# A fused convolution and channel mix: reordering the first bundles of work

## The chip, the cores and the metric

The kernel runs on one core of a Trainium2 chip. A core has five engines that run side by side, each through its own instruction queue in order: TensorE (PE) multiplies matrices and loads their stationary operand (PEld), VectorE (DVE) and ScalarE (ACT) work element by element, GpSimd (POOL) issues most of the loads here, and SyncE (SP) issues the transfers of the results. Sixteen DMA engines move data between HBM and the on-chip memory SBUF. TensorE writes its results into PSUM, which VectorE and ScalarE read.

The metric is the time of one execution on the device in microseconds (us), the median of several runs.

## The reference

The input `x` is `[8, 4160, 192]`: 8 sequences of 4160 positions with 192 channels. First comes a causal convolution along the positions, with 7 taps per head (8 heads of 24 channels), the taps normalised by a softmax. Its result goes through a channel mix:

```python
xk = mu_k * x + (1.0 - mu_k) * x_prev      # x_prev: the position before
xr = mu_r * x + (1.0 - mu_r) * x_prev
k = np.maximum(xk @ w_k, 0.0)              # 192 -> 1024
v = k * k @ w_v                            # 1024 -> 192
r = 1.0 / (1.0 + np.exp(-(xr @ w_r)))      # 192 -> 192
return (r * v).astype(np.float32)
```

Here `x` is already the convolution's result, called `y` below.

## The kernel before

The eight sequences are worked through as four pairs. For each pair the kernel convolves, transposes `y` so that channels lie on partitions (`yT`), mixes, and multiplies.

**Convolution.** Positions are cut into blocks of 120, blocks into groups. Pair 0 has groups 0 to 5 of 3, 4, 4, 5, 10 and 9 blocks; later pairs have four groups each. The convolution is a matmul with a banded matrix `toe`; its input `xb` is loaded by `load_x` through POOL's queue into one of three buffers (`x_tile` takes one). Groups 0 to 2 are convolved whole (`conv_small`: matmuls at L312, copies out of PSUM by ACT at L320). From group 3 on a group is cut into units, each in two halves on TensorE (`conv_mm`, L291); after the second half ACT copies the unit out (`conv_out`, L336). Between the halves ACT's sequencer puts a marker instruction (`clobber_nop`, L299), for which the second half waits.

**Transposing.** Groups 0 to 3 are transposed on TensorE (`tr_first`, and `tr`, L380, four blocks to one PSUM buffer) and copied to `yT` by DVE (L389). From group 4 on `y` goes to HBM (`y_write`, L359) and comes back through a transposing DMA (`y_read`, L367), both in SP's queue.

**Mixing.** A step is a piece of 512 positions of both sequences (256 for the first and the last step of pair 0). `diff` (L433) is the difference of `yT` to its neighbour, `scale` (L464) multiplies one third of the channels by `mu`, `add_y` (L470) adds `yT` again. `mix(s, 0)` gives `xk`, `mix(s, 1)` gives `xr`. All are on DVE, whose order is written out in tables.

**Products.** A step of 512 has eight K slots; a slot is six matmuls (`k_mm`, L490), three thirds of the channels for each of the two sequences, with one block of 128 columns of `w_k` over 512 positions of `xk`, then a ReLU on ACT (`k_relu`, L519) and a square on DVE (`k_square`, L533). A step of 256 has four slots, each covering 256 of the 1024 columns of `w_k`, so slots 0 and 1 of step 0 use columns 0 to 511. For each half step ("quad") there is one R (`r`, 12 matmuls, L564, and a sigmoid on ACT, L572) and one V (`v_rows`, two halves of 32 matmuls, L592), multiplied by `v_out` on DVE (L608) and sent out by SP (L616).

**Order.** Everything stands in an order written out by hand. The K slots are taken four at a time, a *bundle*. `bundle_first` is bundle 0; `bundle_rest` writes the others: four K slots, up to two convolution units, an R and a V of earlier steps. Tables (`early`, `first`, `rq`, `mix_a`, `mix_b`, `mix_c`, `late`) say which other calls stand at which place in which bundle; `run(table, b)` writes them. `at(table, b, fn, ...)` enters a call. Units of group 3 are in bundle 1, of group 4 in bundles 2 and 3, of group 5 in bundles 4 and 5: two per bundle. Later bundles have one unit at most.

PSUM is one ring of four buffers: each K slot, unit, R, V and each transposition of four blocks takes the next buffer, and waits until the buffer's last user has been read out. `xb`, `xk`, `xr` and `k_sb` are rings of three, two, two and four buffers.

The loads at the start stand in POOL's queue in this order: `xb` of group 1, `w_k` in four pieces (`load_wk`: channels 0 to 127 twice, once for each sequence's partitions, then channels 128 to 191 twice), `xb` of groups 2 and 3, `w_r`, `w_v`, then in bundle 1 `xb` of groups 4 and 5.

Of the kernel before, what the change touches and what calls it, by code (L numbers as in the profile page):

```python
# [14 lines left out]
def kernel(  # L15
# [11 lines left out]
    nc = tc.nc  # L27
# [5 lines left out]
    P = 128  # L33
# [65 lines left out]
    def x_tile(g):  # L99
        p, blk0, nb, _, _ = groups[g]  # L100
        xb = three.tile([P, GB, 2, D], BF16, tag="xb", name="xb")
        xbs[g] = xb
        if g > 4:

            nc.vector.memset(xb[0:1, 0, 0, 0:2], 0.0)  # L105
        if blk0 == 0:
            nc.gpsimd.memset(xb[0:32, 0, :, :], 0.0)  # L107
        if blk0 + nb == NBLK:
            nc.gpsimd.memset(xb[:, nb - 1, :, :], 0.0)
# [72 lines left out]
    def load_thirds(w, m, n, cs=slice(0, NC)):  # L182
        for st in range(2):
            nc.gpsimd.dma_start(
                out=w[st * Q : (st + 1) * Q, cs, :],
                in_=bass.AP(
                    tensor=m.tensor,
                    offset=m.offset + cs.start * Q * n,
                    ap=[[n, Q], [Q * n, cs.stop - cs.start], [1, n]],
                ),  # L190
            )

    def load_wk():
        load_thirds(wk, moe_w_k, DF, slice(0, 2))
        load_thirds(wk, moe_w_k, DF, slice(2, 3))

    def load_wr():
        load_thirds(wr, moe_w_r, D)

    def load_wv():  # L200
        nc.gpsimd.dma_start(out=wv, in_=moe_w_v.rearrange("(f p) d -> p f d", p=P))
# [170 lines left out]
    def tr(g, j):  # L372

        p, blk0, nb, _, _ = groups[g]
        ps = ring.tile([P, 2, 2 * BANK], BF16, tag="k", name="ps_t")
        todo = range(4 * j, min(nb, 4 * j + 4))
        view = ps[:, :, 0 : 6 * BLK].rearrange("p b (c i t) -> p b c i t", c=3, i=2)
        for c in range(3):
            for i in todo:
                nc.tensor.transpose(  # L380
                    out=view[:, (i - 4 * j) // 2, c, i % 2, :],
                    in_=ys[g][c][:BLK, i, :] if g < 3 else ys[g][:BLK, i, c * P : (c + 1) * P],
                    identity=ident[:BLK, :BLK],
                )

        for i in todo[::2]:
            n = min(2, nb - i)
            c0 = YC + (blk0 + i) * BLK
            nc.vector.tensor_copy(  # L389
                out=yTs[p][:, :, c0 : c0 + n * BLK].rearrange("p c (n t) -> p c n t", n=n),  # L390
                in_=view[:, (i - 4 * j) // 2, :, :n, :],
            )
# [122 lines left out]
    def k_relu(n):  # L515
        ps = k_ps.pop(n)
        k_sb = four.tile([P, 2 * STEP], BF16, tag="k_sb", name="k_sb")
        k_sbs[n] = k_sb
        nc.scalar.activation(out=k_sb, in_=ps.rearrange("p a b -> p (a b)"), func=AF.Relu)  # L519

    def k_square(n):
        s, j = slots[n]
        L = steps[s][2]
        k_sb = k_sbs.pop(n)
        if j == 0:
            k2s[s] = three.tile([P, NF, 2 * STEP], BF16, tag="k2", name="k2")
        nf = STEP // L
        i = k_sb
        o = k2s[s][:, j, :]
        if nf > 1:  # L530
            i = k_sb.rearrange("p (b f t) -> p f b t", b=2, f=nf)
            o = k2s[s][:, j * nf : (j + 1) * nf, 0 : 2 * L].rearrange("p f (b t) -> p f b t", b=2)
        nc.vector.tensor_tensor(out=o, in0=i, in1=i, op=ALU.mult)  # L533
# [108 lines left out]
    def at(table, b, fn, *a):  # L642
        table.setdefault(b, []).append((fn, a))
# [5 lines left out]
    def conv_half(unit, half):  # L649
        if unit is not None:  # L650
            conv_mm(*unit, half)
            if half == 1:
                conv_out(*unit, nc.scalar.copy)

    for g, (p, blk0, nb, fb, on_pe) in enumerate(groups):
        nx = 1 if g < 3 else len(conv_units(g))
        if g == 0:
            continue
        if g == 1:
            xs = []  # L660
        elif p == 0:
            xs = {2: [0], 3: [1, 1], 4: [2, 2, 3, 3], 5: [4, 4, 5, 5]}[g]
        else:
            xs = range(fb - 10, fb - 10 + nx)
        for i, b in enumerate(xs):
            if g == 2:
                at(late, b, conv, g, i)
            else:
                xt.setdefault(b, []).append((g, i))
        if on_pe:  # L670
            for j in range((nb + 3) // 4):
                at(first, g - 1, tr, g, j)
        else:
            at(late, xs[-1], y_write, g)

            at(late, xs[-1] + (1 if g < 6 else 2), y_read, g)
        if g > 3:

            b = {4: 1, 5: 1, 6: 2, 7: 8}.get(g)
            b = first_bundle[first_step[p]] + (-15, -11, -7, -3)[(g - 6) % 4] if b is None else b  # L680
            at(early, b, x_tile, g)
            at(early, b, load_x, g)
    for s, (p, t0, L, n0, ns) in enumerate(steps):
        fb = first_bundle[s]
        if s == 0:
            at(late, 0, mix, s, 1)
            continue
        if s == 1:
            at(mix_a, 0, diff, s)
            at(mix_a, 0, mix, s, 0)  # L690
            at(mix_a, 1, mix, s, 1)
        else:
            if s == 4:
                at(mix_a, fb - 1, diff, s)
            else:
                at(mix_c, fb - 2, diff, s)
            at(mix_a, fb - 1, scale, s, 0, 0)
            at(mix_b, fb - 1, scale, s, 0, 1, 2)
            at(mix_b, fb - 1, scale, s, 1, 0)
            at(mix_c, fb - 1, add_y, s, 0)  # L700
            at(mix_a, fb, scale, s, 1, 1)
            at(mix_b, fb, scale, s, 1, 2)
            at(mix_b, fb, add_y, s, 1)
        if s == LAST - 1 or s < LAST and steps[s + 1][0] > p:
            at(late, fb - 1, keep_tail, p)
    for s, j, vb in quads:
        at(rq, vb - 1, r, s, j)
        if s == LAST:
            at(late, vb, v_last, s, j)
        else:  # L710
            vq.setdefault(vb, []).append((s, j))

    def run(table, b):
        for fn, a in table.get(b, ()):
            fn(*a)
# [5 lines left out]
    def prologue():  # L721
        nc.sync.dma_start(
            out=w_raw,
            in_=bass.AP(tensor=weight.tensor, offset=weight.offset, ap=[[0, P], [K, H], [1, K]]),
        )
        nc.vector.memset(x_f32[0:32, 0, :, :], 0.0)
        nc.vector.memset(ones_t, 1.0)
        for st in range(2):
            load_x_first(nc.scalar, 0, P, 1, groups[0][2], st, st + 1)
        load_x_first(nc.sync, 16, P, 0, 1, 0, 2)  # L730
        load_mu(0, moe_mu_k)
        load_x_first(nc.scalar, HALO, 16, 0, 1, 0, 2)
        nc.scalar.preload_act_table(AF.Exp)
        nc.vector.memset(zeros, 0.0)  # L734
        x_tile(1)
        nc.gpsimd.affine_select(
            out=ident,
            in_=ones_t,
            pattern=[[1, P]],
            compare_op=ALU.is_equal,  # L740
            fill=0.0,
            base=0,
            channel_multiplier=-1,
        )
        masks_band()
        load_x(1)
        load_wk()

        warm(ring.tile([P, 2, BANK], FP32, tag="k", name="warm"), WARM)
        x_tile(2)  # L750
        masks_mod8()
        softmax()
        make_toe()
        load_x(2)
        load_mu(1, moe_mu_r)
        conv(0, 0)
        tr_first()
        conv(1, 0)
        x_tile(3)
        load_x(3)  # L760
        load_wr()
        load_wv()

    def bundle_first(ns):
# [9 lines left out]
    def bundle_rest(b, ns):  # L774

        units = xt.get(b, []) + [None, None]
        quad = vq.get(b, [None])[0]
        for n in bundles[b - 1][2:] if b > 1 else ():
            k_square(n)
        run(mix_a, b)  # L780
        k_mm(ns[0])
        k_relu(ns[0])
        k_square(ns[0])
        run(mix_b, b)
        conv_half(units[0], 0)
        k_mm(ns[1])
        conv_half(units[0], 1)
        k_relu(ns[1])
        k_square(ns[1])
        run(rq, b)  # L790
        run(first, b)
        if quad:
            v_rows(*quad, 0)
        conv_half(units[1], 0)
        k_mm(ns[2])
        conv_half(units[1], 1)
        k_relu(ns[2])
        if quad:
            v_rows(*quad, 1)
        run(mix_c, b)  # L800
        k_mm(ns[3])
        k_relu(ns[3])
        if quad:
            v_out(*quad)
        run(late, b)
# [51 lines left out]
```

## Time and profile before

| | |
|---|---|
| median of 5 runs | 424.19 us (423.63 to 425.2) |
| profiled execution, its own time | 423.21 us |
| its span, first to last instruction | 421.5 us |
| TensorE busy | 407.5 us, 97% of the span |
| VectorE busy | 380.8 us, 90% |
| ScalarE busy | 347.5 us, 82% |
| chain that ended last, by line | V (L592) 38%, K (L490) 38%, R 7%, convolution 4%, loading `w_k` 2%, reading `yT` back 2% |

How to read it: busy times are those of one profiled execution. The chain that ended last is followed back from the last instruction, at each step to what released it; its shares say where the time went. A wait in brackets after an instruction is idle time of its engine, with the work that ended it. An instruction's line is that of the call that made it, so all K slots have one line. The profiled execution's own time is 1.71 us more than its span.

### The profile page before, as it was taken

The page shows a single profiled execution, that of the slowest core. Times are in us where ns is not written, and L with a number is a line of the kernel's source. Part 1 is how long each engine was busy: PE and PEld are TensorE (multiplying, and loading weights), DVE is VectorE, ACT ScalarE, POOL GpSimd, SP SyncE. Part 2 cuts the span into 40 slices and gives each one's busy share as a digit, 9 for nine tenths or more (in the row PEclk, how much of TensorE's full clock was granted, in tenths as well). Part 3 has the DMA queues.
Part 4 walks back from the last instruction along what each step waited for, and adds up shares of the span by engine and source line. Part 5 has one row for each costly group of instructions (what it writes and reads, how often), then busy time and mean ns, then how long its engine had stood idle before and what let it go on. Part 6 is the DMA issues. An engine that isn't in the chain of part 4 may idle for free.

```text
span 421.5 us, 15786 instructions
## 1 busy us (share of the span) xinstructions
PE 407.5 (97%) x6845; PEld 314.7 (75%) x6845; DVE 380.8 (90%) x678; ACT 347.5 (82%) x407; POOL 48.9 (12%) x73
## 2 busy tenths in 40 slices
PE   6779999999999999999999999999999999999995
PEld 3456768777877787787778777777877787777795
DVE  6897879998999999999999999999999999999983
ACT  5788988888988898888888888988898788777771
POOL 6550001202021010202003010200100000000000
PEclk9999999999999999999999999999999999999999
DMA  8997779959589793887869794695756484421123
GB/s 132 192 178 114 183 187 184 206 186 176 165 147 222 147 213 118 139 198 159 192 110 213 170 193 136 136 237 142 151 145 138 139 157 121 117 78 53 64 79 113
DMA packets 134502, 64.58 MB, mean 153 GB/s; under 512 B 85132, under 2 KB 134048, under 8 KB 134432
## 3 DMA queue, kind: packets, MB, share of 16 engines
q1 hardware_dynamic: 96050, 48.31, 44.6%
q0 software_dynamic: 37488, 14.66, 30.4%
q8 instruction: 53, 0.87, 0.9%
q10 hardware_dynamic: 894, 0.61, 0.5%
q14 instruction: 17, 0.14, 0.1%
HBM read 29.92 MB, written 36.99 MB: 159 GB/s over the span
## 4 chain that ended last, share of the span: by engine, by line
PE 89%; DVE 4%; DMA 4%; ACT 1%; POOL 1%; issue 1%; SPq 0%; ACTq 0%; DVEq 0%
PE ps_v L592 38%; PE ps_k L490 38%; PE ps_r L564 7%; PE ps_c L291 4%; DMA wk<-in_moe_w_k_dram 2%; DMA yT<-y_dram 2%; PE ps_v L547 1%; DVE k L533 1%; ACT k_sb L519 1%; DVE d L433 0%; DVE yT L389 0%; DVE xk L470 0%; DVE xk L464 0%; POOL xb L125 0%; DVE xr L464 0%
## 5 line engine op out<-in xcount | busy, mean ns | idle before, releaser
L519 ACT ACTIVATE k_sb<-ps_k 128x1024 bf16<-128x1024 f32 x260 | 260.9, 1038 | 55.5 <-PE ps_k L490 55.3
L490 PE MATMUL ps_k<-xk,wk 64*128 64x512 bf16 (+1 forms) x1632 | 200.9, 367 | 2.9 <-DVE xk L470 1.6
L533 DVE TENSOR_TENSOR k<-k_sb 128x1024 bf16<-128x1024 bf16 x260 | 177.7, 688 | 14.0 <-ACT k_sb L519 6.4
L592 PE MATMUL ps_v<-wv,k 64*128 64x192 bf16 x4032 | 188.8, 243 | 0.6 <-ACT k_sb L519 0.6
L592 PEld LDWEIGHTS <-k 64*128 64x128 bf16 x4032 | 172.4, 94 | 13.2 <-issue 0.6
L490 PEld LDWEIGHTS <-wk 64*128 64x128 bf16 x1632 | 87.1, 94 | 55.0 <-DVE xk L470 2.3
L608 DVE TENSOR_TENSOR o_sb<-ps_v,r_sb 128x768 f32<-128x768 f32 x64 | 61.2, 957 | 13.5 <-PE ps_v L592 9.0
L572 ACT ACTIVATE r_sb<-ps_r 128x768 bf16<-128x768 f32 x65 | 54.6, 840 | 0.0
L336 ACT CAST y<-ps_c 120x960 bf16<-120x960 f32 (+4 forms) x67 | 50.9, 787 | 4.3 <-PE ps_c L291 4.3
L125 POOL DMA_DIRECT2D xb<-in_x_dram x34 | 30.8, 909 | 196.8 <-PE ps_c L291 129.2
L564 PEld LDWEIGHTS <-xr 64*128 64x128 bf16 x780 | 36.0, 94 | 12.8 <-DVE xb L105 2.0
L564 PE MATMUL ps_r<-wr,xr 64*128 64x192 bf16 x780 | 43.8, 243 | 1.7 <-DVE xb L105 1.7
L291 PE MATMUL ps_c<-xb,toe 64*128 64x480 bf16 (+2 forms) x240 | 39.4, 335 | 0.0
L464 DVE TENSOR_SCALAR xr<-d,mu 128x512 bf16<-128x512 bf16 (+1 forms) x102 | 35.2, 348 | 0.0
L464 DVE TENSOR_SCALAR xk<-d,mu 128x512 bf16<-128x512 bf16 (+1 forms) x99 | 32.4, 356 | 0.1
L470 DVE TENSOR_TENSOR xr<-xr,yT 128x1536 bf16<-128x1536 bf16 (+1 forms) x33 | 31.0, 939 | 1.1
L433 DVE TENSOR_TENSOR d<-yT 128x1536 bf16<-128x1536 bf16 (+2 forms) x35 | 31.1, 888 | 0.8 <-DMA yT<-y_dram 0.6
L470 DVE TENSOR_TENSOR xk<-xk,yT 128x1536 bf16<-128x1536 bf16 (+1 forms) x32 | 30.2, 944 | 0.0
L291 PEld LDWEIGHTS <-toe 64*128 64x128 bf16 x240 | 13.3, 94 | 11.9 <-issue 0.3
L417 POOL COPY y_tail<-yT 128x195 bf16<-128x195 bf16 x4 | 1.8, 457 | 68.6 <-DMA yT<-y_dram 68.6
L719 PE MATMUL warm<-zeros,ones_t 128*128 128x512 bf16 x16 | 5.0, 480 | 1.8 <-DVE zeros L734 1.8
L107 POOL MEMSET xb<- 32x384 bf16 x3 | 1.2, 407 | 45.9 <-PE ps_k L490 43.7
(54 smaller groups left out, 64.0 us busy)
## 6 DMA issues: line engine op xcount, KB each, us to landing
out_dram<-o_sb SPq DMA_DIRECT2D x128, 192.0 KB, 2.9
y_dram<-y SPq DMA_DIRECT2D x10, 900.0 KB, 6.7
xb<-in_x_dram POOLq DMA_DIRECT2D x14, 480.0 KB, 8.9
xb<-in_x_dram POOLq DMA_DIRECT2D x6, 432.0 KB, 7.6
xb<-in_x_dram POOLq DMA_DIRECT2D x10, 192.0 KB, 5.0
y_dram<-y SPq DMA_DIRECT2D x3, 450.0 KB, 5.8
y_dram<-y SPq DMA_DIRECT2D x1, 810.0 KB, 6.0
xb<-in_x_dram POOLq DMA_DIRECT2D x2, 384.0 KB, 7.0
```

The source lines that it names most:

```text
L291: nc.tensor.matmul(out=banks[:, bank, :, :, k * G : (k + 1) * G], lhsT=toe[q, h, :], rhs=xbs[g][q, :nb, :, h * G : (h + 1) * G], start=hal ...
L336: copy(out=bass.AP(tensor=y.tensor, offset=y.offset + d0, ap=[y.ap[0], [d1 - d0, 2], [2 * D, nb], [Q, 2], [1, n]],), in_=bass.AP(tensor=ps ...
L433: nc.vector.tensor_tensor(out=shaped(s, diffs[s][:, cs, :L]), in0=y_of(s, cs, 1), in1=y_of(s, cs, 0), op=ALU.subtract)
L464: nc.vector.tensor_scalar(out=t[:, c, :L], in0=diffs[s][:, c, :L], scalar1=mu[:, i, c : c + 1], scalar2=None, op0=ALU.mult)
L470: nc.vector.tensor_tensor(out=o, in0=o, in1=y_of(s, sl, 0), op=ALU.add)
L490: nc.tensor.matmul(out=ps[:, i, f * L : (f + 1) * L], lhsT=wk[r, c, fs], rhs=xk[r, c, :L], start=c == 0 and f == 0, stop=c == NC - 1 and f ...
L519: nc.scalar.activation(out=k_sb, in_=ps.rearrange("p a b -> p (a b)"), func=AF.Relu)
L533: nc.vector.tensor_tensor(out=o, in0=i, in1=i, op=ALU.mult)
L564: nc.tensor.matmul(out=ps[:, i, k * D : (k + 1) * D], lhsT=xr[q, c, ts], rhs=wr[q, c, :], start=c == 0, stop=c == NC - 1,)
L572: nc.scalar.activation(out=r_sbs[s, j], in_=ps[:, :, 0 : 2 * D], func=AF.Sigmoid)
L592: nc.tensor.matmul(out=v_ps[s, j][:, bank, k * D : (k + 1) * D], lhsT=k2s[s][q, f, t * P : (t + 1) * P], rhs=wv[q, f, :], start=half == 0 ...
L608: nc.vector.tensor_tensor(out=o_sb.rearrange("p (b t) d -> p b (t d)", b=2), in0=v_ps.pop((s, j)), in1=r_sbs.pop((s, j)), op=ALU.mult,)
```

## The change

Six edits, all of which touch the start of the program and bundles 0 to 8.

- `load_wk` loads `w_k` by halves of its columns: two pieces for columns 0 to 511 (all 192 channels, once for each sequence's partitions), then two for columns 512 to 1023.
- Group 4's `x_tile` and `load_x` move from bundle 1 to the start, ahead of `load_wv`. Group 7's move from bundle 8 to bundle 7.
- `tr` writes its transposes in pairs of blocks, all three channel parts of a pair together. For group 1 the second pair is copied to `yT` by ACT instead of DVE.
- The table `first` (the transposes of groups 2 and 3) is run behind the first K slot and its ReLU instead of behind the second slot and R.
- Up to bundle 6, an R stands in the bundle of its V instead of one bundle earlier, so that bundle 6 holds two R. The mixes for R of steps 0, 1 and 2 stand later, those of step 1 in parts.
- Where a bundle has two units, the third of its K slots with its ReLU moves ahead of the second unit, and the second half of that unit behind V's second half.

```diff
     def load_wk():
-        load_thirds(wk, moe_w_k, DF, slice(0, 2))
-        load_thirds(wk, moe_w_k, DF, slice(2, 3))
+        for half in range(2):
+            h = slice(half * DF // 2, (half + 1) * DF // 2)
+            for st in range(2):
+                nc.gpsimd.dma_start(
+                    out=wk[st * Q : (st + 1) * Q, :, h],
+                    in_=bass.AP(
+                        tensor=moe_w_k.tensor,
+                        offset=moe_w_k.offset + h.start,
+                        ap=[[DF, Q], [Q * DF, NC], [1, DF // 2]],
+                    ),
+                )
...
-        for c in range(3):
-            for i in todo:
-                nc.tensor.transpose(
...
+        for i0 in todo[::2]:
+            for c in range(3):
+                for i in range(i0, min(nb, i0 + 2)):
+                    nc.tensor.transpose(
...
         for i in todo[::2]:
...
-            nc.vector.tensor_copy(
+            copy = nc.scalar.copy if g == 1 and i > 0 else nc.vector.tensor_copy
+            copy(
...
-        if g > 3:
-
-            b = {4: 1, 5: 1, 6: 2, 7: 8}.get(g)
+        if g > 4:
+
+            b = {5: 1, 6: 2, 7: 7}.get(g)
...
         if s == 0:
-            at(late, 0, mix, s, 1)
+            at(mix_c, 1, mix, s, 1)
             continue
         if s == 1:
             at(mix_a, 0, diff, s)
             at(mix_a, 0, mix, s, 0)
-            at(mix_a, 1, mix, s, 1)
+            at(mix_a, 1, scale, s, 1, 0)
+            at(mix_b, 1, scale, s, 1, 1)
+            at(late, 2, scale, s, 1, 2)
+            at(late, 2, add_y, s, 1)
         else:
-            if s == 4:
+            if s == 2:
+                at(mix_b, 1, diff, s)
+            elif s == 4:
                 at(mix_a, fb - 1, diff, s)
             else:
                 at(mix_c, fb - 2, diff, s)
             at(mix_a, fb - 1, scale, s, 0, 0)
             at(mix_b, fb - 1, scale, s, 0, 1, 2)
-            at(mix_b, fb - 1, scale, s, 1, 0)
             at(mix_c, fb - 1, add_y, s, 0)
-            at(mix_a, fb, scale, s, 1, 1)
+            if s == 2:
+                at(mix_a, fb, scale, s, 1, 0)
+                at(mix_b, fb, scale, s, 1, 1)
+            else:
+                at(mix_b, fb - 1, scale, s, 1, 0)
+                at(mix_a, fb, scale, s, 1, 1)
             at(mix_b, fb, scale, s, 1, 2)
             at(mix_b, fb, add_y, s, 1)
...
     for s, j, vb in quads:
-        at(rq, vb - 1, r, s, j)
+        at(rq, vb if vb < 7 else vb - 1, r, s, j)
...
         load_wr()
+        x_tile(4)
+        load_x(4)
         load_wv()
...
         k_mm(ns[0])
         k_relu(ns[0])
+        run(first, b)
         k_square(ns[0])
...
         run(rq, b)
-        run(first, b)
         if quad:
             v_rows(*quad, 0)
+        k_mm(ns[2])
+        k_relu(ns[2])
         conv_half(units[1], 0)
-        k_mm(ns[2])
-        conv_half(units[1], 1)
-        k_relu(ns[2])
         if quad:
             v_rows(*quad, 1)
+            conv_half(units[1], 1)
         run(mix_c, b)
         k_mm(ns[3])
+        if not quad:
+            conv_half(units[1], 1)
         k_relu(ns[3])
```

More of the change, by code (lines that the diff above doesn't have):

```diff
@@ L377, in tr @@
         view = ps[:, :, 0 : 6 * BLK].rearrange("p b (c i t) -> p b c i t", c=3, i=2)
-        for c in range(3):
-            for i in todo:
-                nc.tensor.transpose(
[L381 to L384, printed above, removed]
+        for i0 in todo[::2]:
+            for c in range(3):
+                for i in range(i0, min(nb, i0 + 2)):
+                    nc.tensor.transpose(
+                        out=view[:, (i - 4 * j) // 2, c, i % 2, :],
+                        in_=ys[g][c][:BLK, i, :] if g < 3 else ys[g][:BLK, i, c * P : (c + 1) * P],
+                        identity=ident[:BLK, :BLK],
+                    )
         for i in todo[::2]:
```

## The prediction

> **What bounds the kernel now.** I read the first part of the page, then busy time by stretches, then TensorE's waits, then the chain and the timeline of the first 65 us.
>
> ```profile
> span 421.5 us, 15786 instructions
> PE 407.5 (97%) x6845; PEld 314.7 (75%) x6845; DVE 380.8 (90%) x678; ACT 347.5 (82%) x407; POOL 48.9 (12%) x73
> ```
>
> TensorE is busy in 97% of the span. The stretches (columns: PE, PEld, DVE, ACT, POOL busy us with counts, granted clock, DMA share, GB/s) show where the rest is:
>
> ```profile
> 15.00:20.00 5.00, 3.85 (x54) 2.30 (x48) 4.90 (x9) 5.00 (x8) 2.63 (x4) 1.00 1.60 191
> 20.00:25.00 5.00, 3.28 (x50) 1.98 (x44) 4.93 (x14) 3.91 (x6) 2.39 (x3) 1.00 1.60 192
> 25.00:30.00 5.00, 3.63 (x45) 2.31 (x44) 4.74 (x11) 5.00 (x7) 2.86 (x5) 1.00 1.58 190
> 60.00:65.00 5.00, 4.46 (x74) 3.00 (x70) 4.96 (x10) 3.81 (x5) 0.00 (x0) 1.00 0.58 170
> 70.00:80.00 10.00, 10.00 (x185) 8.04 (x182) 9.36 (x18) 8.75 (x11) 3.71 (x5) 1.00 1.31 182
> ```
>
> From 65 us to the tail TensorE never rests, so a change in the first bundles shows in the time only as the shift of the last place where TensorE waits, at 61.65 us. Between 15 and 30 us VectorE is full and TensorE starves. Its waits up to 60 us, from the list of waits:
>
> ```profile
> PE ps_r L564 <- DVE xb L105: 1.7, 1, 1.7
> PE ps_k L490 <- DVE xk L470: 1.0, 1, 1.0
> PE ps_k L490 <- DVE yT L389: 0.7, 1, 0.7
> PE ps_v L592 <- ACT k_sb L519: 0.6, 1, 0.6
> PE ps_k L490 <- DMA wk<-in_moe_w_k_dram: 0.6, 1, 0.6
> ```
>
> The 1.7 us is R standing in TensorE's queue until its mix is added up (the add, 0.56 us from 21.32, ends at 21.88; R starts at 21.94). The chain shows two transfers ahead of TensorE's work:
>
> ```profile
> 4.62 7.92 DMA wk<-in_moe_w_k_dram
> 12.58 1.04 PE ps_k L490 x15
> ...
> 49.63 7.73 DMA yT<-y_dram
> 57.38 0.97 DVE d L433
> ...
> 61.65 0.82 PE ps_k L490 x6
> ```
>
> **The change part by part.** Timeline rows give the units. Start to start: a K slot 0.65, half a V 1.32, half a conv unit 0.20, an R 0.49, a ReLU 0.92, a scale 0.30, a square 0.62, a yT copy on DVE 0.53, a diff or add of 1536 columns 0.97. The rows that matter most for ACT are:
>
> ```profile
> 14.73 3.77 ACT L519 ACTIVATE k_sb<-ps_k 128x1024 bf16<-128x1024 f32 x4 [2.41 <-PE ps_k L490]
> 18.36 1.60 ACT L320 CAST y_small<-ps_c 120x512 bf16<-120x512 f32 x3
> 21.94 0.67 PE L564 MATMUL ps_r<-wr,xr 64*128 64x192 bf16 x12 [1.72 <-DVE xb L105]
> 25.82 0.82 PE L490 MATMUL ps_k<-xk,wk 64*128 64x512 bf16 x6 [0.67 <-DVE yT L389]
> ```
>
> *1. K weights by halves.* K slots 0 and 1 need columns 0 to 511 only. The pieces still number four, but the first two carry 384 KB instead of 512. The x ahead of them ends at 10.3 (conv of group 1 stops waiting for it at 10.34), and the queues move 205 to 207 GB/s from 9 to 12 us: 10.3 + 384/205 = 12.15, against 12.54. The last pieces come at the same time as before. Bounds: no gain if the shorter rows cost as much as they save, 128/205 = 0.6 us at most. I take 0.4, since both rates come from this very stretch. [...]
>
> *2. Transposes of group 1.* K's first two thirds run 12.15 to 13.2, 12 transposes (0.75) to 13.95. The two yT copies were 0.97 on DVE. Now the second is on ACT, and in the built program its only wait is on DVE's counter, so it runs behind the first. No row shows this copy on ACT; its bounds are 0.46 (360 columns, the first block's copy) and 1.02 (a ReLU of 1024); by width, between 0.60 for 512 and 0.84 for 768, I take 0.77. So 13.95 + 0.53 + 0.77 = 15.25, diff 16.25, scales 17.15, add 18.15, K slot 4 at 18.2 against 18.34: 0.15 of the 0.4 is left. ACT pays: its ReLUs start at 15.25 instead of 14.73, so the three casts of group 2 end at 20.5 instead of 19.96.
>
> *3. Bundle 1.* R (0.49) and the wait of 1.72 leave, and so does the wait of 0.67 behind DVE's queue. DVE's mix of step 0 for R (three scales 0.67, add 0.56) and most of R's mix of step 1 (1.85) move behind squares. But the transposes of group 2 now stand right behind slot 4 (18.2 to 18.85) and wait for the casts: done at about 21.0, some 1.5 us of new wait. From there: half unit 0.20, slot 5 0.65, half unit 0.20, slot 6 0.65, half unit 0.20, a wait of about 0.35 for a PSUM buffer, slot 7 0.65, half unit 0.20 give 24.1, and slot 8 starts there, against 25.82.
>
> *4. Bundle 2.* The transposes of group 3 stand behind slot 8 (to 24.75) and wait for ACT, which has from 20.5: ReLU 0.92; the copy of the first unit (0.97, ready at 22.1) to 23.1; two ReLUs to 24.9; two copies (1.02) to 25.9. Transposes to 26.75, half unit. Slot 9 needs a buffer that the ReLU of slot 8 frees at 27.7. Slot 9, half unit, R: 0.65 + 0.20 + 0.49, V at 29.15 against 30.16. That is 1.0 us earlier, but with one R fewer behind it: 0.5 of real lead.
>
> *5. The deferred R.* Bundles 3 to 5 then hold one R each, as before, at the period of 6.7. Bundle 6 holds two (the row `vb < 7`): 0.49 more, and with two sigmoids of 0.84 in ACT's queue V may wait for a buffer: between 0 and 0.84, I take 0.4, half. V of bundle 6: 57.00 - 1.0 + 0.49 + 0.4 = 56.9.
>
> *6. The y chain.* SP's queue keeps its order: outputs of bundle 3, y write (42.93), outputs of bundle 4, transposing read (49.63). All follow V, so all move 1.0 earlier: landing at 56.36 instead of 57.36, and K of step 4 at 61.65 - 1.0 = 60.65. TensorE is free for it 3.93 after V of bundle 6 begins (60.93 - 57.00 before): 56.9 + 3.93 = 60.85. The later of the two holds: 61.65 - 60.85 = 0.8, and some 0.1 more, since K's weight load waited 1.04 there and TensorE's tail is in the 0.55. **Sum: 0.9 us.**
>
> *7. Costed at nothing.* Group 4's x (2 x 480 KB) stands ahead of the V weights: at 190 GB/s these land 5.05 us later than 13.82 + 7.4 = 21.2, at 26.3, covered by V's start at 29.15. Without that cover each us would be paid in full. Group 4's x lands about 2.0 earlier (384 KB less ahead), near 24.3; its conv asks at 26.8, where the old order (26.3) would have been tight. The scale of step 3's xr in bundle 4 now waits for the R of that bundle; behind it stand squares, and the add that bundle 5 needs. The corresponding rows before are R ending at 43.7 and that scale at 44.71, so 1 us is to spare. Group 7's memset (0.06 on DVE) and loads go one bundle earlier; no stage near asks for them. The second half of conv units behind V's second half gives ACT's marker 1.32 us more; nothing waits there today.
>
> The granted clock stays 1.00 in the stretch that holds a wait of 1.72; no new wait is longer, so nothing is added for the clock.
>
> **The rivals.** (a) *No gain:* the halves bring nothing (0.4 lost in step 2), or bundle 6 waits the full 0.84: 0.3 to 0.5 remain, about 423.8. For it: ACT is 5.00 of 5.00 busy from 15 to 20 us, and takes more work. Against: VectorE is unloaded exactly there. (b) *More:* ACT's copies and TensorE's waits in bundles 1 and 2 are shorter than I placed (1.5 + 1.1 + 0.7 us of waits are mine, no row shows them); with 0.8 of them gone V and the y chain move with them: 1.7 gained, 422.5. Against: each hangs on a full ACT. (c) *Slower:* ACT's chain from 14.5 to 27.7 is the new bound, since TensorE's in-order queue now has transposes ahead of K slots. If the copy on ACT, or the order of its copies, is 1.0 us longer than placed, the gain is gone; each further us costs one. At 1.9 us longer the result is 425.2. The widest ACT row, 1.02, says this needs more than one copy to be late. (d) *The change doesn't move the end:* the landing of yT varies by itself (median 7.2, here 7.73). If it lands within 7.0 of its issue, the wait at 61.65 is gone in both kernels, and 60.93 - 60.85 = 0.1 is left: 424.1. It is counted in (a).
>
> **How the numbers follow.** The profiled execution took 423.21 us, 1.71 outside its span; the sum makes that 422.3. The median of five is 424.19, 0.98 above it (423.63 to 425.2), and 424.19 - 0.9 = 423.3 is the forecast. Chances: the forecast (0.6 to 1.3 gained) 0.48, (a) with (d) 0.14, (b) 0.28, (c) 0.10. A measurement can tell 0.2% (0.85 us) from no change. The forecast falls about 0.28 on the faster side and 0.20 within; with (b) faster is 0.56, with (a) the same is 0.34, slower 0.10. Range: 2.2 gained, (b) with all its waits and the 0.6 of step 1, gives 422.0; (c) at 1.4 us late gives 424.6.
>
> **What would show it.** First K matmul in earnest near 12.15. Slot 4 near 18.2. ACT's copy of yT as a row of 0.77. New waits of TensorE's transposes on ACT at 19 to 20.5 and 25 to 26, none of R at 21.9. V's first start near 29.15. Two R back to back near 56. The read of yT landing near 56.4, and no wait, or 0.2, at step 4's K slot. Wrong if V starts after 30.2, if V's weights land after it, or if TensorE waits anywhere past 65 us.

## The result and the profile after

The changed kernel took 423.11 us (median of 31 runs, 421.87 to 424.26), the kernel before 424.41 us beside it (52 runs, 422.93 to 426.32): a ratio of 0.997, with a 95% interval of 0.996 to 0.9979. The gain is 1.3 us (0.9 to 1.7 by the interval). The forecast was 0.9 us and 423.3 us.

The profiled execution of the changed kernel took 424.04 us, near the top of its runs, and its span is 0.8 us longer than that of the kernel before. The first part of its page:

```profile
span 422.3 us, 15787 instructions
PE 409.9 (97%) x6845; PEld 315.1 (75%) x6845; DVE 381.1 (90%) x677; ACT 347.8 (82%) x408; POOL 49.0 (12%) x73
```

Its stretches, in the columns of the stretches shown for the kernel before:

```profile
15.00:20.00 5.00, 3.14 (x32) 1.65 (x31) 4.82 (x9) 5.00 (x8) 2.23 (x4) 1.00 1.59 191
20.00:25.00 5.00, 4.41 (x50) 2.36 (x48) 4.77 (x12) 4.07 (x6) 2.31 (x3) 1.00 1.60 192
25.00:30.00 5.00, 3.84 (x59) 2.69 (x61) 4.70 (x13) 3.89 (x6) 3.57 (x5) 1.00 1.58 188
60.00:65.00 5.00, 4.55 (x77) 3.08 (x73) 4.97 (x10) 3.77 (x5) 1.88 (x2) 1.00 0.49 129
```

TensorE gains 1.13 us of work between 20 and 25 us (3.28 to 4.41) and loses 0.71 between 15 and 20 us (3.85 to 3.14). ScalarE is full from 15 to 20 us, as before. TensorE's longest waits in its list of waits, up to 65 us and after its warm-up:

```profile
PE ps_k L501 <- DVE xk L481: 0.9, 2, 0.5
PE ps_t L390 <- ACT y_small L329: 0.8, 3, 0.4
PE ps_t L390 <- ACT y L345: 0.7, 2, 0.4
PE ps_k L501 <- ACT k_sb L530: 0.5, 1, 0.5
PE ps_c L321 <- ACT k_sb L530: 0.5, 1, 0.5
PE ps_k L501 <- DMA wk<-in_moe_w_k_dram: 0.4, 1, 0.4
```

R's wait of 1.7 is gone. What stands in its place are waits on ScalarE: its casts of the convolution (`y_small`, `y`) and its ReLUs (`k_sb`). The rows of the timeline at the places that the prediction named (start, duration, engine, line, what, and in brackets the idle time before and what ended it):

```profile
11.93 1.04 PE L501 MATMUL ps_k<-xk,wk 64*128 64x256 bf16 x15 [0.41 <-DMA wk<-in_moe_w_k_dram]
14.32 0.76 ACT L400 COPY yT<-ps_t 128x720 bf16<-128x720 bf16 x1 [2.39 <-DVE yT L400]
14.97 3.78 ACT L530 ACTIVATE k_sb<-ps_k 128x1024 bf16<-128x1024 f32 x4
18.04 0.82 PE L501 MATMUL ps_k<-xk,wk 64*128 64x512 bf16 x6 [0.47 <-DVE xk L481]
18.60 1.61 ACT L329 CAST y_small<-ps_c 120x512 bf16<-120x512 f32 x3
24.00 0.82 PE L501 MATMUL ps_k<-xk,wk 64*128 64x512 bf16 x6
27.68 0.82 PE L501 MATMUL ps_k<-xk,wk 64*128 64x512 bf16 x6 [0.54 <-ACT k_sb L530]
...
49.51 4.10 SPq L376 DMA_TRANSPOSE yT<-y_dram  x1
55.35 1.38 PE L575 MATMUL ps_r<-wr,xr 64*128 64x192 bf16 x24
56.91 1.50 PE L603 MATMUL ps_v<-wv,k 64*128 64x192 bf16 x32 [0.18 <-ACT y L345]
61.47 0.82 PE L501 MATMUL ps_k<-xk,wk 64*128 64x512 bf16 x6 [0.45 <-DVE xk L481]
```

The first V begins at 29.14 (30.16 before; 29.15 was forecast), the V of bundle 6 at 56.91 (57.00; 56.9). Up to there the working holds to a tenth. But K of step 4 begins at 61.47, only 0.18 before the 61.65 of the kernel before, where 0.8 was forecast: the read of `yT` went out at 49.51, not at 48.6. The experiments show what stood in its way, and a part of why the median gained 1.3 us all the same.

### The profile page after: what moved, and what is told of

Its sections match the earlier page's. It is cut to its first block, busy times and chain, and to the rows that moved or that the text cites. A ratio compares the mean times of both kernels' runs of the same rounds, so it can differ in the third digit from the quotient of the medians.

```text
span 422.3 us, 15787 instructions
## 1 busy us (share of the span) xinstructions
PE 409.9 (97%) x6845; PEld 315.1 (75%) x6845; DVE 381.1 (90%) x677; ACT 347.8 (82%) x408; POOL 49.0 (12%) x73
## 4 chain that ended last, share of the span: by engine, by line
PE 89%; ACT 2%; DVE 2%; issue 1%; ACTq 0%; DVEq 0%
PE ps_v L603 39%; PE ps_k L501 37%; PE ps_r L575 7%; PE ps_c L300 4%; ACT k_sb L530 2%; PE ps_v L558 1%; DVE o_sb L619 1%; ACT y L345 0%; DVE d L444 0%; DVE k L544 0%; DVE yT L400 0%; DVE xk L481 0%; DVE xr L475 0%; PE ps_t L390 0%; DVE o_sb L639 0%
## 5 line engine op out<-in xcount | busy, mean ns | idle before, releaser
L300 PEld LDWEIGHTS <-toe 64*128 64x128 bf16 x240 | 13.4, 94 | 12.2 <-DVE o_sb L619 0.5
L739 PE MATMUL warm<-zeros,ones_t 128*128 128x512 bf16 x16 | 6.6, 598 | 1.8 <-DVE zeros L754 1.8
L739 PEld LDWEIGHTS <-ones_t 128*128 128x128 bf16 x19 | 2.5, 134 | 5.8 <-issue 4.1
```

The lines of the kernel that those rows point to most:

```text
L300: nc.tensor.matmul(out=banks[:, bank, :, :, k * G : (k + 1) * G], lhsT=toe[q, h, :], rhs=xbs[g][q, :nb, :, h * G : (h + 1) * G], start=hal ...
```

## The experiments

Landmarks in the tables below: *K* is the first K matmul behind the weights, *V1* the first V, *V7* the V of bundle 7, behind the last place where TensorE waits for a mix. Each execution is listed with the mean clock that was granted to TensorE; "clock fell" counts those at 0.996 or less, for the reason shown in the first experiment. The groups ran on different chips, each beside its own runs of the kernel before (medians 424.07 to 424.41).

| kernel | ratio (95%) | median, runs | median without the fall | clock fell | K | V1 | V7 |
|---|---|---|---|---|---|---|---|
| before | 1 | 424.19 (80) | 424.12 | 7 of 80 | 12.58 | 30.16 | 63.86 |
| changed | 0.997 (0.996 to 0.9979) | 423.11 (55) | 422.91 | 18 of 55 | 11.93 | 29.14 | 63.67 |
| halves alone | 1.0001 (0.9986 to 1.0016) | 424.13 (10) | 424.13 | 0 of 10 | 11.40 | 30.07 | 64.45 |
| no halves | 1.000 (0.9986 to 1.0015) | 424.07 (10) | 423.88 | 2 of 10 | 12.25 | 29.75 | 63.65 |
| R early | 1.000 (0.9981 to 1.0018) | 424.20 (10) | 423.18 | 4 of 10 | 11.45 | 29.85 | 63.06 |
| transposes late | 0.9964 (0.9948 to 0.9979) | 422.62 (7) | 422.62 | 0 of 7 | 11.92 | 28.73 | 62.78 |
| x late | 0.9982 (0.9966 to 0.9998) | 423.36 (12) | 422.73 | 6 of 12 | 11.90 | 30.52 | 64.42 |
| copy on VectorE | 0.995 (0.9932 to 0.9968) | 421.87 (14) | 421.68 | 1 of 14 | 11.86 | 28.17 | 62.07 |
| y first | 0.9983 (0.9965 to 1.0) | 423.46 (12) | 422.75 | 6 of 12 | 11.61 | 28.85 | 62.76 |
| y first and copy | 0.9963 (0.9949 to 0.9976) | 422.39 (8) | 422.39 | 0 of 8 | 11.62 | 28.01 | 62.58 |

(The 55 executions of the changed kernel are those of three groups; the 80 of the kernel before are those listed beside the experiments. The ratio of the copy on VectorE is that of its second group. The landmarks are those of one profile each; x late's is one in which the clock fell.)

**Both kernels once more.** The kernel before, unedited:

> The kernel before, unchanged, for a second profile of the y chain. Theory: first V at 30.2, V of bundle 6 at 57.0, and step 4's K slot at 4.3 us behind the landing of yT, wherever that lands; if the y write takes 7.5 us here too, the slot is at 62.4 and the lead of the changed kernel is whole again. Rival: slot at 61.6 with the same landing as in the first profile, and the lead at this place is 0.2 us in every profile.

Measured: 423.1 us, K at 12.32, V1 at 29.89, V7 at 63.56, everything some 0.3 earlier than in the first profile of this kernel from the first K on. The order of its waits is the same, and K of step 4 begins 4.30 behind the landing of `yT` (57.06), as expected. Two profiles of one kernel differ by 0.3 us at the start.

The changed kernel, unedited, twice:

> The changed kernel once more, unchanged, for a second profile. Theory (the lead of the first V is worth 1.0 us, and the end moves by whichever is later at step 4's K slot: the y chain or TensorE's own queue): first V at 29.1, V of bundle 6 at 56.9, step 4's K slot between 60.6 and 61.5 as the y write takes 6.7 or 7.5 us; ratio to the kernel before 0.996 to 0.998. Rival (the early lead is lost in the y chain, and the gain comes from elsewhere): step 4's K slot at 61.5 again, and the ratio is 0.997 all the same.

> The changed kernel itself once more, beside the others of this group. If the parts work together (each left out alone cost the whole gain), the ratio is 0.997 again (423.1) while the kernels without the halves and with R early, measured at 1.000, stay above it. If instead the three ratios differ only by the scatter of single executions, this one falls between 0.997 and 1.000. In the profile: first V 29.0 to 29.3 at a full clock; the second output of bundle 4 issued by SP in 0.45 us (then the read of yT near 48.7 to 49.0 and V of bundle 7 near 63.1) or in 1.3 to 1.6 (then 49.5 and 63.7); a stall of TensorE near 113 us of 0.5 to 0.7, or none, by whether the 16 KB block of its code starts to load some 13 us or 11 us after the block before it.

Measured: 0.9969 (0.9952 to 0.9985), 423.11 us, and 0.9976 (0.9961 to 0.9991), 423.13 us. The gain repeats. But V1 stands at 30.74 and 31.24 in these two profiles, 1.6 and 2.1 us later than in the first. Of this 0.3 and 0.7 stand at slot 4 already (18.32 and 18.72 for 18.04). Two stretches of the first of them and two rows of its timeline show what the rest is (the third figure from the end of a stretch is the granted clock):

```profile
16.57:19.98 3.41, 1.84 (x18) 0.72 (x15) 3.38 (x8) 3.41 (x6) 0.98 (x2) 1.00 1.60 191
19.98:23.40 3.42, 3.24 (x24) 1.85 (x26) 2.80 (x9) 1.43 (x3) 2.31 (x3) 0.50 1.60 191
```

```profile
20.05 1.47 PE L390 MATMUL ps_t<-ident,y_small 120*128 120x120 bf16 x10 [0.21 <-ACT y_small L329]
21.83 1.49 PE L501 MATMUL ps_k<-xk,wk 64*128 64x512 bf16 x6
```

The clock falls to 0.50 for 3.41 us just behind the stretch in which TensorE waits most, and a K slot's matmuls, 0.81 us in the first profile, take 1.49. It fell at 19.98, 20.60 and 20.17 us in three of five profiles (these two and x late's; not in the changed kernel's first and in y first's), though but for the order of two loads in x late their kernels are the same up to there. 1.71 us of full clock lost in a span of 422 lowers the mean by 0.004, so a mean of 0.996 or less marks such an execution. The tail has its own half-clock stretch (the last 1.54 us of the changed kernel's first profile, 0.002 of its mean clock), so the mark is not exact. By it the clock fell in 18 of 55 executions, with a median of 423.89 against 422.91 of the others.

**The K weights alone, and all but the K weights.** Halves alone puts the new `load_wk` into the kernel before; no halves puts the old one into the changed kernel:

```
-        for half in range(2):
-            ...
+        load_thirds(wk, moe_w_k, DF, slice(0, 2))
+        load_thirds(wk, moe_w_k, DF, slice(2, 3))
```

> The kernel before with the K weights by column halves and nothing else. Theory (step 1 was right in size, and alone it reaches V): K in earnest at 11.9 to 12.1 against 12.3 to 12.6, step 4's gate moved by the same 0.4 to 0.6; first V near 29.6 against 29.9 to 30.2, V of bundle 7 near 63.4; time 0.4 to 0.6 lower, near 423.9, ratio 0.9985 to 0.999. Rival 1 (rows of 1 KB cost what the smaller share saves): K at 12.5, ratio 1.000. Rival 2 (without the second queue for the copies the gain is eaten by DVE, which bounds 15 to 30 us): K at 12.0, but first V still at 30.0 and ratio 1.000.

> The changed kernel with the K weights in the old pieces (512 KB, then 256 KB for each half of the rows). Theory: K in earnest at 12.4, everything up to first V 0.4 to 0.8 later than in the changed kernel (29.6 to 30.0), V of bundle 7 near 64.2, and the time about 0.5 above the changed kernel's 423.1: 423.6, ratio to the kernel before 0.998. So the halves are a third to half of the whole gain. Rival (the gain comes from bundles 1 to 3 and the halves are absorbed at the step-4 gate): first V at 29.2, ratio 0.997 as for the changed kernel.

Measured: halves alone brings nothing (1.0001), though K begins at 11.40 and slot 4 at 17.47 instead of 18.34. The theory's first V (29.6) was missed; V1 and the ratio are the second rival's, but not for its reason. The timeline in bundles 1 and 2:

```profile
19.49 0.38 PE L300 MATMUL ps_c<-xb,toe 64*128 64x240 bf16 x4 [1.20 <-DMA xb<-in_x_dram]
21.06 0.67 PE L573 MATMUL ps_r<-wr,xr 64*128 64x192 bf16 x12 [0.34 <-DVE xb L105]
...
26.86 0.38 PE L300 MATMUL ps_c<-xb,toe 64*128 64x480 bf16 x2 [1.09 <-DMA xb<-in_x_dram]
...
30.07 0.67 PE L601 MATMUL ps_v<-wv,k 64*128 64x192 bf16 x12 [0.58 <-ACT k_sb L528]
```

At group 3's x TensorE already waits 1.20, but R's wait shrinks for it (0.34 for 1.72), and slot 8 still begins 0.87 earlier (24.95). Then the convolution of group 4 asks for its x before it is there (it lands at 26.73, behind the V weights), and TensorE waits 1.09 us for it. The time saved at the front is lost at a later transfer of the same queue. In the changed kernel this convolution stands behind transposes and asks only at 26.76; x late, below, loses no time that can be told apart with the x at 26.47. Left out of the changed kernel, the halves cost the whole gain (1.000), and 1.0 us among the executions without the fall (423.88 against 422.91); in the profile K and V1 come 0.3 and 0.6 later. V7 doesn't show it (63.65 against 63.67), since the changed kernel's first profile lost time in between.

**R early.** Each R of the first bundles one bundle ahead of its V, and its mixes where they were:

```
-        at(rq, vb if vb < 7 else vb - 1, r, s, j)
+        at(rq, vb - 1, r, s, j)
         (and the mixes for R of steps 0, 1 and 2 where the kernel before has them)
```

> The changed kernel with each R of the first bundles and its mixes back where they were (R one bundle ahead of its V, mix of step 0 in bundle 0, of step 1 whole in bundle 1); halves, order of loads, paired transposes and their new place stay. Theory (the deferral takes 1.7 us of R's wait out of bundle 1 and is the largest part of the change): TensorE waits 1.5 to 2 us for the mix again, first V at 30.1 or later against 29.1, V of bundle 6 then follows without the double R: about 57.0, V of bundle 7 near 63.8; time about 0.4 above the changed kernel's, 423.5, ratio 0.998 to 0.999. Rival (the wait of R was cover for waits on ACT that come anyway): first V at 29.1 to 29.4, no double R later, and a time 0.3 to 0.5 below the changed kernel's, ratio 0.996.

Measured: V1 at 29.85, V of bundle 6 at 56.76 without a double R, V7 at 63.06. The waits of R are not 1.5 to 2: R itself runs at 21.49 without one, and TensorE waits behind it:

```profile
21.49 0.66 PE L575 MATMUL ps_r<-wr,xr 64*128 64x192 bf16 x12
22.70 0.82 PE L501 MATMUL ps_k<-xk,wk 64*128 64x512 bf16 x6 [0.56 <-ACT y L345]
23.94 0.38 PE L300 MATMUL ps_c<-xb,toe 64*128 64x240 bf16 x4 [0.41 <-DVE yT L400]
```

So the first V is 0.7 later with R early, though slot 4 begins 0.37 earlier (17.67), and the V of bundle 6 is 0.15 ahead: the double R there takes back most of what the deferral gave. Neither the theory's waits nor the rival's first V came. The ratio (1.000) speaks for the deferral, the executions without the fall (423.18 against 422.91, six of them) and the profile hardly do. What the deferral brings lies between nothing and about 1 us, and stays open.

**Transposes late.** The transposes of groups 2 and 3 back behind R's place, and step 2's diff with them:

```
         k_relu(ns[0])
-        run(first, b)
 ...
         run(rq, b)
+        run(first, b)
```

> The changed kernel with the transposes of groups 2 and 3 back behind R's place, and step 2's diff one slot later, as before the change; the rest as changed. Theory (the transposes ahead of K slots trade R's wait for waits on ACT and bring little by themselves): the waits of 0.8 and 0.7 of the transposes on ACT's casts shrink, first V at 28.9 to 29.1, time within 0.3 of the changed kernel. Rival (their place is what keeps VectorE fed in bundle 1, so that slot 8 can start): VectorE gets yT of group 2 some 1.5 us later, slot 8 waits for the diff and its scales, first V at 29.8 or later, time 0.5 to 1.0 above the changed kernel's.

Measured: 0.9964, 422.62 us (beside it the changed kernel had 423.13, or 422.98 without the fall), and V1 at 28.73, under the forecast's 28.9. Of the transposes' 1.5 us of waits on ScalarE 0.2 is left; in their place stand 0.55 at a K slot and 0.61 at V, both for ReLUs. The diff of step 2 comes at 25.62 instead of 23.05 without a wait of TensorE for it. The theory holds: the new place brought nothing, and at V1 it costs 0.4.

**x late.** Group 4's x behind the V weights, the rest as changed:

```
         load_wr()
+        load_wv()
         x_tile(4)
         load_x(4)
-        load_wv()
```

> The changed kernel with the fifth group's x behind the V weights again. Theory (costed at nothing, with 1.9 us of cover lost for the conv): the V weights land near 21.5, the x near 26.5; the conv that reads it begins at 26.8 in the changed kernel, so it waits 0 to 0.3, first V 29.1 to 29.4, the time that of the changed kernel within 0.3. Rival 1 (that order was part of the gain): conv of the fifth group waits for its x by 0.5 to 1.0, first V near 30, 0.5 to 1.0 slower. Rival 2 (loads of V's weights late in the new order slow the start): first V earlier than 29.0.

Measured: 423.36 us, 422.73 among the executions without the fall, where the changed kernel has 422.91: no difference that this tells apart. The x lands at 26.47, the V weights at 21.31. In its profile the clock had fallen, so the convolution asked only at 28.1; the profile can't show a wait at 26.8. In the kernel with the copy on VectorE, next, it asks at 25.79, where an x at 26.47 would be late by 0.7; that was not run.

**The copy on VectorE.** Both copies of `yT` of group 1 on VectorE, twice:

```
-            copy = nc.scalar.copy if g == 1 and i > 0 else nc.vector.tensor_copy
+            copy = nc.vector.tensor_copy
```

> The changed kernel with group 1's second yT copy back on DVE. Theory (ACT's chain bounds bundles 1 and 2, and its copy of 0.76 us stands at the head of that chain): ReLUs start 0.5 to 0.7 us earlier, the first V near 28.3 instead of 29.14, V of bundle 6 near 56.1; time 0.4 to 1.0 us below the changed kernel. Rival (DVE bounds there, and the copy on ACT relieves it): the first V at 29.1 or later, time the same or 0.2 to 0.5 us above the changed kernel.

> The changed kernel with both yT copies of group 1 on VectorE, once more. Theory (ACT's chain from 15 to 27 us sets the first V, and the copy on ACT lengthens it by 0.5 to 1.0): first V near 28.1, one us ahead of the changed kernel, and a ratio of 0.994 to 0.995, faster than the changed kernel beside it by 0.8 to 1.3 us. Rival (the first measurement of 6 runs was lucky, and the us is absorbed at the y gate of step 4): first V near 28.1 all the same, V of bundle 7 near 63.2, and the ratio of the changed kernel, 0.997.

Measured: 0.9942 (0.9921 to 0.9963), 421.9 us, and 0.995 (0.9932 to 0.9968), 421.87 us; beside it the changed kernel had 423.11 and 423.13. It is the fastest kernel of the study, 1.2 us ahead of the changed one. Its timeline, of the second run:

```profile
14.01 3.77 ACT L530 ACTIVATE k_sb<-ps_k 128x1024 bf16<-128x1024 f32 x4 [2.03 <-PE ps_k L501]
17.64 1.60 ACT L329 CAST y_small<-ps_c 120x512 bf16<-120x512 f32 x3
17.88 0.82 PE L501 MATMUL ps_k<-xk,wk 64*128 64x512 bf16 x6 [1.07 <-DVE xk L481]
19.30 0.59 PE L390 MATMUL ps_t<-ident,y_small 120*128 120x120 bf16 x8 [0.21 <-ACT y_small L329]
28.17 1.07 PE L603 MATMUL ps_v<-wv,k 64*128 64x192 bf16 x22
```

The ReLUs begin at 14.01 instead of 14.97, the casts at 17.64 instead of 18.60, and the first V 0.97 earlier. All of ScalarE's 0.96 reaches V; 0.07 of it was there at K. Slot 4, for whose diff the copy was moved off VectorE, begins at 17.88 instead of 18.04: with both copies on one engine it isn't even later. The 1.07 that TensorE waits there costs nothing: the last eight transposes behind slot 4 begin at 19.30, when ScalarE's casts end (17.64 + 1.60), as they begin at 20.27 in the changed kernel, whose casts end at 20.21. This edit together with the transposes late, the other edit with a lower median than the changed kernel, was not run.

**y first.** Group 4's `y_write` ahead of bundle 3's outputs in SP's queue; then both edits together:

```
-            at(late, xs[-1], y_write, g)
+            at(ylate if g == 4 else late, xs[-1], y_write, g)
 ...
         k_relu(ns[3])
+        run(ylate, b)
         if quad:
             v_out(*quad)
```

> The changed kernel with group 4's y write ahead of bundle 3's outputs in SP's queue. Theory (step 4's K slot waits for yT, whose read waits for the landing of the y write): the write is issued near 40.8 instead of 42.06, yT lands 1.0 to 1.3 us earlier, TensorE's wait of 0.45 us at step 4's K slot is gone or under 0.2, time 0.2 to 0.5 us below the changed kernel. Rival (the read waits for SP's queue or the DMA rate): yT lands at 57.2 as before and the time is the same.

> Both of the earlier edits together: the second yT copy back on VectorE, and the fifth group's y written ahead of bundle 3's outputs in SP's queue. Theory (two bounds in a row: ACT's chain up to the first V, then the y chain at step 4): first V at 28.1 as with the copy alone; y write issued near 40 and its read near 47, so that K of step 4 waits for nothing; V of bundle 7 at 61.5 to 62.0; time 0 to 0.5 below the copy's 421.9, ratio 0.993 to 0.9945. Rival (writing y first only moves a wait that no longer binds, and delays the outputs): as with the copy alone or up to 0.4 worse, ratio 0.994 to 0.995 .

Measured: y first removes the wait at step 4's K (the V of bundle 7 follows that of bundle 6 by 6.14 us, 56.62 to 62.76, against 6.76 in the changed kernel's first profile), but the ratio is 0.9983: the clock fell in 6 of its 12 executions (424.33 against 422.75). Without the fall the 422.75 is no better than the 422.66 of the changed kernel beside it, whose second and third profiles have 6.14 there too. Together with the copy it is no better than the copy alone (ratio 0.9963 against 0.995), and the wait is back:

```profile
60.38 0.82 PE L501 MATMUL ps_k<-xk,wk 64*128 64x512 bf16 x6 [0.49 <-DVE xk L481]
```

Its `y` was in HBM at 46.51, yet the read went out at 48.27. SP issues the two outputs of bundle 4 ahead of it, and the second took 1.44 us to issue instead of 0.45. The same happened in the changed kernel's first profile. SP's rows in the timeline of the changed kernel and of the one before:

```profile
47.44 1.98 SPq L627 DMA_DIRECT2D out_dram<-o_sb  x2
49.51 4.10 SPq L376 DMA_TRANSPOSE yT<-y_dram  x1
```

```profile
48.65 0.89 SPq L616 DMA_DIRECT2D out_dram<-o_sb  x2
49.63 4.19 SPq L367 DMA_TRANSPOSE yT<-y_dram  x1
```

The outputs are 1.21 us earlier and take 1.09 longer to issue, and so the read leaves at nearly the same time. The long issue at this place was in 3 of the 14 profiles (halves alone too, 1.30). It is not rare: in every profile, of both kernels and all variants, SP takes over 1 us to issue 8 to 12 of the 132 outputs (11 in the changed kernel's first profile), and what differs is which of them. In two of the three it ends 7.4 us after the `y` write was issued, where the read that waits for that write otherwise leaves after 6.6 to 6.7; in y first and copy the write had landed by then. Its cause stays open.

**What was not taken out alone.** The transposes in pairs, the new order of K slots and convolution units, and group 7's earlier x have no run of their own. Taken out one at a time, the halves cost the first V 0.6 and the deferred R 0.7, while the transposes' new place and the copy on ScalarE give back 0.4 and 1.0: together about nothing, against the 1.02 that the whole change gained there. Either the parts don't add up, or those without a run hold the rest; no run tells which.

## Why the prediction was right, and where it was not

**Step 1, the halves: too small.** 0.4 was taken, 0.65 came (12.58 to 11.93), just past the bound of 0.6. The sum took a KB for 1000 bytes; with 1024 it comes to 0.3, and its bound to 0.64. The other profiles agree: the second piece of the weights landed at 12.20 to 12.54 in the three without the halves and at 11.35 to 11.88 in the eleven with them. The working held the x ahead of the weights fixed, but it landed at 9.46 in the changed kernel's first profile and at 10.21 in the kernel before, so that the 0.65 isn't the halves' alone. No slowdown by the shorter rows shows in K's start (11.40 to 11.93 in the table with the halves, 12.25 and 12.58 without). The step didn't say that in the old order the gain is lost at group 4's x; the halves alone showed it.

**Step 2, the copy on ScalarE: right in time, wrong in worth.** The row was put at 0.77 and is 0.76; slot 4 was put at 18.2 and is at 18.04. But "ACT pays" was sized at 0.52, against the kernel before, whose ReLUs started later because its weights came later. Against the same kernel with the copy on VectorE it is 0.96: there the first ReLU begins at 14.01, while here ScalarE stands idle until 14.32, since its copy waits for VectorE's, and the first ReLU begins 0.65 after the copy does. All of it goes to the first V, and the medians differ by 1.2. This is the largest thing that the working didn't see: it asked what the copy costs against before, not what it costs against its other place.

**Steps 3 and 4: right, the last digit by luck.** Waits of 1.5 and 1.1 us on ScalarE's casts were forecast, 0.8 and 0.7 came. The places they end were right: slot 8 at 24.00 for 24.1, slot 9 at 27.68 for 27.7, V at 29.14 for 29.15. From slot 9 on, though, the step's own terms come to 29.04, not 29.15; the half unit took 0.32 and not 0.20, and the two errors cancel.

**Step 5: right at V, a little different inside.** Two R back to back at 55.35, V at 56.91 for 56.9. V's wait is 0.18 and not 0.4.

**Step 6 failed in the profile.** "All follow V, so all move 1.0 earlier" held for the `y` write (42.06, 0.87 earlier) and for the first output of bundle 4 (47.44, 1.21 earlier), and broke at the second, which SP took 1.54 us to issue. `yT` landed at 57.17 for 56.36, K of step 4 waited 0.45 and started at 61.47 for 60.85. Where SP issued in 0.45 us, as in the changed kernel's other two profiles and in the one with the transposes late (read at 48.45, landed at 55.97), that wait is gone, and the V of bundle 7 follows that of bundle 6 by 6.14 us, TensorE's own time (58.51 to 64.65, 59.01 to 65.15, 56.64 to 62.78). With it the V of the changed kernel's first profile would stand at 56.91 + 6.14 = 63.05, 0.81 earlier than before; the step had 0.8 for this term.

**Step 7 held.** The V weights landed at 26.50 for 26.3, group 4's x at 24.47 for 24.3, and nothing waited for either. The sentence on the clock did not hold: "no new wait is longer, so nothing is added for the clock". None was longer, and yet the clock fell in about a third of the executions. By the medians this adds 0.2 us (422.91 to 423.11). One of the signs of being wrong came too: TensorE stood still past 65 us, once, for 0.55 ahead of 114.39 (last section).

**The sum** of 0.9 stands against a measured 1.3, and the profiles hold only about half of that: 0.8 at the V of bundle 7 when SP issues in time, less 0.2 for the clock. The other 0.7 is open, so that the median came this near to the forecast is in part luck. Both profiles of the kernel before are of executions well below its median (423.21 and 423.1, against 424.07 to 424.41), and no profile shows what the others do. The halves alone, which have that kernel's order, show what can happen: with a long issue by SP (V7 at 64.45) and a stop of 0.46 near 113 us their profiled execution took 424.71. Whether the kernel before does the same is not shown. The changed kernel's first profile has the opposite luck: beside the late issue it lost 0.7 us between 94 and 155 us (61.30 from V to V for 60.57), 0.55 of it in the stop that the last section shows, and 0.3 behind TensorE's last matmul.

**The rivals.** (c), ScalarE as the new bound, is the mechanism that is really there: ScalarE's chain sets the first V, and moving 0.76 us of work off it brought 0.97 there and 1.2 in the median. It did not decide, because the working had already put 0.77 for the copy on ScalarE's path; nothing there was longer than placed. (b), waits on ScalarE shorter than placed, came true for the waits (1.5 for 2.6) and not for the places: slots 8 and 9 and the first V stood where they were put. (d), the landing of `yT`, took 7.66 us and not 7.0 or less; it varies (7.40 to 7.81 in the 14 profiles), but never came under 7.0, and what held the read was its issue.

## What to carry to other kernels

When a piece of work is moved from a full engine to another, price it at both places in the new order, not against the old order: here the second copy delayed nobody on VectorE, and on ScalarE everything behind it, by 0.96 us. The earlier K weights helped here only as far as the next transfer of the same stretch was early too, or was asked for late enough (with the halves alone TensorE waited 1.09 us for group 4's x); look for who asks next in the queue. And where a single profile and the median disagree, list every execution's clock before looking for a reason in the order of the work.

## What was not expected of the hardware

**The clock.** In three profiles it fell to 0.50 for 3.41 us, each time 13.65 us after it had first risen, which is four times 3.41. (It rose at 4.57 us in the first profile of the kernel before: the warm-up matmuls start 0.43 us apart ahead of that, and 0.21 behind.) TensorE was busy in 1.84 of the 3.41 us ahead of one fall (the stretch shown above). A stretch of the halves alone, 16.91 to 20.32 us, had 1.66, and its clock stayed; the stretch of the kernel before that holds most of R's wait had as little as the first, and its clock stayed too:

```profile
18.22:21.64 3.42, 1.88 (x20) 0.89 (x20) 3.39 (x9) 3.42 (x7) 0.44 (x1) 1.00 1.61 191
```

So the busy time of such a stretch alone doesn't tell whether the clock falls. Nor does busy time sort the kernels: from 15 to 20 us TensorE is busier with the copy on VectorE (3.27 of 5 us) and with the transposes late (3.68) than in the changed kernel's first profile (3.14), and those two fell in 1 of 21 executions, the changed kernel in 18 of 55. But the changed kernel's third profile has 3.27 and fell, and the halves alone have the least (2.62) and fell in 0 of 10. What sets it off stays open.

**A stop of TensorE.** In 8 of the 14 profiles TensorE stood still once for 0.25 to 0.66 us near 113 us, at the same matmul, 20 of 32 into half a V, and the profile shows nothing that it waited for (`issue`). From the changed kernel's timeline:

```profile
114.39 0.67 PE L603 MATMUL ps_v<-wv,k 64*128 64x192 bf16 x12 [0.55 <-issue]
```

The trace has transfers of the program itself, on a queue of the kind `instruction`: 53 blocks of 16 KB. The block at this place landed at 113.06, 1.3 us before the matmul that went on; in the eight profiles it starts to load 12.6 to 13.1 us after the block before (13.09 in this one), in the other six 10.8 to 12.2 (11.03 in the first profile of the kernel before). That TensorE waited for this block is not shown, and neither is what delays its load. The stop costs up to 0.66 us, as large as the effects that this study set out to tell apart.
